# A gated recurrence and a mixture of experts on one core: products read in token order, row scatters freed of each other, and a new order table

## The chip, the cores and the metric

The kernel is one program on one core of a Trainium2 chip. The metric is the device time of one execution in microseconds; lower is better. The engines are named as the profile names them: PE (matmul; PEld is its weight load), DVE (vector), ACT (scalar), POOL (GpSimd) and SP (sync, which here issues most transfers).

## The reference

```python
# attention block: batch 4, 8 heads, 768 tokens, head size 48, float32
mag = sqrt(a_re*a_re + a_im*a_im); scale = minimum(mag, 0.999) / (mag + 1e-6)
a = (a_re + 1j*a_im) * scale                      # one complex gate per token, head and channel
for t in range(S):                                # state: 48 x 48 per batch and head
    St = a[t][:, None] * St + outer(k[t], v[t])
    y[t] = q[t] @ real(St)
x = y.transpose(0, 2, 1, 3).reshape(3072, 384)    # token rows
# experts: 8 experts, 384 -> 1024 -> 384, one expert per token, no token dropped
e = argmax(x @ w_gate, axis=1); g = softmax(x @ w_gate)[e]
out[n] = g[n] * (maximum(x[n] @ w1[e[n]], 0) @ w2[e[n]])
```

## The kernel before

**Attention.** The recurrence is computed in 24 blocks of 128 tokens: `u` counts the six chunks of the sequence, `b` the four batches, and a loop runs over `g = u*4 + b`. Once per `u`, logarithms, arctangents and two products with a triangular matrix (`csl`, `cst`) turn the gates into decays and rotations. Per block, `products` makes the rotated queries and keys `Q` and `K` on DVE; `scores` turns them on PE (`tp`), copies them out on ACT (`kt`, `qt`), multiplies them (`at`) and masks the result on DVE (`am`); `outer` and `state` keep the running state `G`; `results` adds two products for each head in the PSUM tile `yt`: `v` times `am`, and from the second chunk on `G` times `qt`. `evict` copies `yt` to `ys` on ACT, `finish` turns `ys` in 32 by 32 squares on DVE into `x`, and four transfers on SP's queue write `x` to the DRAM scratch `xd`, one row for each token. `logits` and `pick_logits` multiply `ys` with the gate weights.

**How `results` uses PE.** Two heads share a column of `yt`: head `i=0` writes partitions 0 to 47, head `i=1` partitions 64 to 111. The moving operand is a row of 128 tokens. It is read through

```python
def by_square(t):
    return t.rearrange("p (s j) -> p j s", j=CT)      # CT = 4
```

so that column `j*32+s` of `yt` is token `s*4+j` of the block, and the operand's consecutive reads lie four float32 apart. `at`, `tp` and all products of the experts read their moving operand without a gap. Since the columns stand in that order, so do the partitions of `lg`, `tid1` and `xid1`, and `finish` writes partition `s` to the rows `s*4 .. s*4+3`. A float32 matmul of the program shows as two MATMUL instructions in the trace: 192 calls with `am` are x384 in a row.

**Routing.** After chunk pairs, `route` ranks the tokens of each expert and sums their token numbers (`tid1`, `xid1`) into `slots`. `first_place` finds the expert with the most tokens (product `cnt`), after which SP loads that expert's `wa` and `wb`, and POOL gathers its first 256 rows `xg` from `xd`. Its first half (`hps`, `yps`) is computed while the last chunk is routed.

**Experts.** Each of eight experts takes its rows by indirect gathers on POOL, multiplies with `wa` (`hx`, `hy`, `hz`, `hv`, and `mx` to `mv` for the second product), scales by the gate into `y`, and `scatter` writes each `y` of up to 128 rows to `out` by one indirect transfer on POOL. There are 28 scatters and a last one. All write to the tensor `out`, so the framework puts them one after another: each waits for the landing of the one before. `drain` puts a POOL drain behind the scatters of experts 3 and 6, and later scatters behind it. The last `y` is held back: at the end every engine reads a flag and branches over a fallback path (the `If` at line 1282), then DVE scales the last 104 rows (`y<-mv,gate`) into a tile of the pool `lasty`, and the last scatter (`out_dram<-y,lasts`) ends the kernel.

**What sets the order.** All engine calls up to the end of the attention part are recorded (a helper at line 110 issues them, so all have that line). `ORDER` gives for each engine the sequence in which they run, as numbers of the recorded calls; the loop at line 1190 ties each to the next on its engine. The experts' part is ordered by the program and by chains of `behind`.

Of the kernel before, what the change touches and what calls it, by code (L numbers as in the profile page):

```python
# [48 lines left out]
    """,  # L49
    "scalar": """  # L50
# [9 lines left out]
    """,  # L60
    "vector": """
# [15 lines left out]
    """,  # L77
    "gpsimd": """
        3 21 17 7 0 18 16 6 11 25 23 13 1 19 10 20 9 2 26 5 4 28 22 27 29 12 30+1 14 32 34 8 33 35+1 38 24 40 15 37 39
        42 44 41 43 46 45 47+1  # L80
    """,
    "sync": """
# [48 lines left out]
def kernel(  # L131
# [42 lines left out]
    def behind(ins, others, reason="order"):  # L174
        for o in others:
            tc.add_manual_dep(ins.ins, o.ins.name, NOSYNC, reason=reason)
# [38 lines left out]
    tid1 = const([P, NU, B], "tid1")  # L215
    xid1 = const([P, NU, B], "xid1")
    for t, pattern in ((tid1, [[P, NU], [S, B]]), (xid1, [[B * P, NU], [P, B]])):
        for a in range(CT):
            nc.gpsimd.iota(
                t[a * Q4 : (a + 1) * Q4], pattern=pattern, base=1 + a, channel_multiplier=CT,  # L220
                allow_small_or_imprecise_dtypes=True,
            )
# [238 lines left out]
    def by_square(t):  # L461
        return t.rearrange("p (s j) -> p j s", j=CT)

    def results(u, b, hg):
        half, c = divmod(b, HB)
        V = T["v", u, half][:, c]
        for hp in range(2 * hg, 2 * hg + 2):
            o = [yt[i * 64 : i * 64 + D, hp].rearrange("p (j s) -> p j s", j=CT) for i in range(2)]
            for i in range(2):
                mm(o[i], V[:, 2 * hp + i], by_square(T["am", u, b, hg][:, 2 * (hp % 2) + i]), True, u == 0)  # L470
            for i in range(2):
                if u > 0:
                    mm(o[i], T["G", b][0:DD, 2 * hp + i], by_square(T["qt", u, b, hg][0:DD, 2 * (hp % 2) + i]), False, True)
# [20 lines left out]
    def finish(u, b):  # L494

        x = ch.tile([P, CT, Q4, HP], FP, tag="x", name="x")
        nc.vector.transpose(
            out=x.rearrange("p j s i -> p i j s"), in_=T["ys", u, b].rearrange("p i (j s) -> p i j s", j=CT)
        )
        rows = xd[(u * B + b) * P : (u * B + b + 1) * P, :].rearrange("(s j) c -> s j c", j=CT)  # L500
        for a in range(4):
            w = min(Q4, D - a % 2 * Q4)
            c0 = a // 2 * D + a % 2 * Q4
# [1065 lines left out]
```

## Time and profile before

| | |
|---|---|
| median of three runs | 567.14 us (561.68 to 567.54) |
| profiled execution | 566.88 us; span 565.1 us, that is 1.8 us around the span |
| PE | 537.3 us busy, 95% of the span |
| DVE | 384.0 us, 68% |
| ACT | 257.0 us, 45% |
| POOL | 173.4 us, 31% |
| mean granted TensorE clock | 0.991 |

Attention takes about the first 293 us: up to 40 us the first gates are loaded and turned, from 43.4 us on `yt` is written. The first half of the first expert follows to about 323 us, the rest of the experts to 553 us, and a tail without matmuls to 565 us. Matmuls are pipelined: the mean time of one contains its way through the array, and two neighbours overlap. What a matmul costs is read from starts, or from the busy time of a group divided by its count.

### The profile page before, as it was taken

The page shows a single profiled execution, that of the slowest core. Times are in us where ns is not written, and L with a number is a line of the kernel's source. Part 1 is how long each engine was busy: PE and PEld are TensorE (multiplying, and loading weights), DVE is VectorE, ACT ScalarE, POOL GpSimd, SP SyncE. Part 2 cuts the span into 40 slices and gives each one's busy share as a digit, 9 for nine tenths or more (in the row PEclk, how much of TensorE's full clock was granted, in tenths as well). Part 3 has the DMA queues.
Part 4 walks back from the last instruction along what each step waited for, and adds up shares of the span by engine and source line. Part 5 has one row for each costly group of instructions (what it writes and reads, how often), then busy time and mean ns, then how long its engine had stood idle before and what let it go on. Part 6 is the DMA issues. An engine that isn't in the chain of part 4 may idle for free. (4 is left out here: it accounts for less than half of the span.)

```text
span 565.1 us, 9630 instructions
## 1 busy us (share of the span) xinstructions
PE 537.3 (95%) x3626; PEld 427.2 (76%) x3626; DVE 384.0 (68%) x754; ACT 257.0 (45%) x424; POOL 173.4 (31%) x174
## 2 busy tenths in 40 slices
PE   4699999999999999999999999999999999999991
PEld 3487777777787867766758678888888989898990
DVE  4599776787898797777726527677576666665730
ACT  6797868574686875553321013232323313232320
POOL 1050120040031012000010566777538346146322
PEclk9999999999999999999999999999999999999997
DMA  9949667465753465331081197465453637371111
GB/s 166 172 67 135 133 116 142 76 108 103 143 93 71 75 131 78 69 73 29 16 267 29 41 369 273 158 223 185 134 213 111 245 134 265 128 252 42 42 56 40
DMA packets 173646, 73.51 MB, mean 130 GB/s; under 512 B 153677, under 2 KB 168039, under 8 KB 172696
## 3 DMA queue, kind: packets, MB, share of 16 engines
q1 hardware_dynamic: 168504, 63.05, 46.5%
q0 software_dynamic: 5088, 9.77, 5.7%
q8 instruction: 30, 0.49, 0.4%
q14 instruction: 24, 0.20, 0.1%
HBM read 63.30 MB, written 9.68 MB: 129 GB/s over the span
## 5 line engine op out<-in xcount | busy, mean ns | idle before, releaser
L110 POOL DMA_INDIRECT xg<-xd,tok x92 | 104.5, 1136 | 119.2 <-DVE am L110 64.7
L110 POOL TENSOR_SCALAR carry<-fg 32x768 f32<-32x768 f32 x10 | 23.9, 2392 | 176.2 <-DVE fg L110 176.0
L110 PE MATMUL yt<-am,v 128*48 128x128 f32 x384 | 67.9, 407 | 0.0
L110 PE MATMUL yt<-qt,G 96*48 96x128 f32 x320 | 62.5, 407 | 0.0
L110 POOL DMA_INDIRECT out_dram<-y,row x28 | 31.7, 1133 | 82.7 <-DMA out_dram<-y,row 25.3
L110 PEld LDWEIGHTS at<-qt,kt 96*128 96x128 f32 x384 | 47.4, 191 | 9.4 <-issue 6.0
L110 PE MATMUL at<-qt,kt 96*128 96x128 f32 x384 | 53.4, 281 | 0.2 <-ACT qt L110 0.2
L110 DVE TENSOR_TENSOR am<-at,tri 128x512 f32<-128x512 f32 x48 | 32.9, 685 | 22.3 <-PE at L110 19.5
L110 PE MATMUL mv<-wb,ht 128*128 128x384 f32 (+5 forms) x176 | 43.2, 488 | 0.0
L110 PEld LDWEIGHTS yt<-qt,G 96*48 96x48 f32 x320 | 28.8, 139 | 13.7 <-issue 1.7
L110 PEld LDWEIGHTS yt<-am,v 128*48 128x48 f32 x384 | 26.6, 132 | 15.2 <-issue 5.6
L110 ACT COPY kt<-tp 96x512 f32<-96x512 f32 x48 | 27.9, 582 | 18.9 <-PE tp L110 18.8
L110 ACT COPY qt<-tp 96x512 f32<-96x512 f32 x48 | 28.0, 583 | 16.4 <-PE tp L110 14.9
L110 PEld LDWEIGHTS mv<-wb,ht 128*128 128x128 f32 (+5 forms) x176 | 22.3, 156 | 15.8 <-issue 4.6
L110 PEld LDWEIGHTS dk<-v,K 128*96 128x96 f32 x320 | 30.1, 165 | 2.8 <-issue 1.9
L110 PE MATMUL dk<-v,K 128*96 128x48 f32 x320 | 30.8, 246 | 0.0
L110 PE MATMUL tp<-ident,Q 128*96 128x128 f32 x192 | 30.1, 276 | 0.5 <-ACT qt L110 0.2
L110 PE MATMUL tp<-ident,K 128*96 128x128 f32 x192 | 30.5, 276 | 0.0
L110 ACT ACTIVATE ht<-hv 128x192 f32<-128x192 f32 (+6 forms) x18 | 8.3, 461 | 46.1 <-PE hv L110 46.1
L110 DVE STREAM_TRANSPOSE x<-ys 128x512 f32<-128x512 f32 x24 | 26.7, 1114 | 3.2 <-ACT ys L110 3.1
L110 PE MATMUL hx<-xt,wa 128*128 128x192 f32 (+5 forms) x136 | 28.4, 334 | 0.2 <-DVE xt L110 0.2
L110 ACT COPY ys<-yt 128x512 f32<-128x512 f32 x24 | 14.1, 587 | 27.1 <-PE yt L110 27.1
(238 smaller groups left out, 1156.0 us busy)
## 6 DMA issues: line engine op xcount, KB each, us to landing
wb<-in_moe_w_dram SPq DMA_DIRECT2D x8, 1536.0 KB
wa<-in_moe_w_dram SPq DMA_DIRECT2D x7, 1536.0 KB
k<-in_k_dram SPq DMA_DIRECT2D x12, 384.0 KB
v<-in_v_dram SPq DMA_DIRECT2D x12, 384.0 KB
q<-in_q_dram SPq DMA_DIRECT2D x12, 384.0 KB
rc<-in_a_re_dram SPq DMA_DIRECT2D x6, 768.0 KB
rc<-in_a_im_dram SPq DMA_DIRECT2D x6, 768.0 KB
ar<-in_a_re_dram SPq DMA_DIRECT2D x9, 384.0 KB
```

Of the source, the lines that this page charges most:

```text
L110: ins = f(*a, **kw)
```

## The change

Five things change together.

1. `by_square` is gone: `results` reads `am` and `qt`, and writes `yt`, in the natural order of tokens. Column `j*32+s` is token `j*32+s`.
2. `finish` writes partition `s` of `x` to the rows `s`, `32+s`, `64+s`, `96+s` of the block. The pieces have the same sizes as before. `tid1` and `xid1` are made by one `iota` each instead of four.
3. All scatters are declared free of dependence on one another (a group "rows"). In the fallback path a drain waits for all of them.
4. The fallback path reads its rows in the same natural order.
5. `ORDER` is replaced for all five engines; its numbers name other calls where calls fell away.

```diff
-            o = [yt[i * 64 : i * 64 + D, hp].rearrange("p (j s) -> p j s", j=CT) for i in range(2)]
+            o = [yt[i * 64 : i * 64 + D, hp] for i in range(2)]
             for i in range(2):
-                mm(o[i], V[:, 2 * hp + i], by_square(T["am", u, b, hg][:, 2 * (hp % 2) + i]), True, u == 0)
+                mm(o[i], V[:, 2 * hp + i], T["am", u, b, hg][:, 2 * (hp % 2) + i], True, u == 0)
             for i in range(2):
                 if u > 0:
-                    mm(o[i], T["G", b][0:DD, 2 * hp + i], by_square(T["qt", u, b, hg][0:DD, 2 * (hp % 2) + i]), False, True)
+                    mm(o[i], T["G", b][0:DD, 2 * hp + i], T["qt", u, b, hg][0:DD, 2 * (hp % 2) + i], False, True)
...
-        rows = xd[(u * B + b) * P : (u * B + b + 1) * P, :].rearrange("(s j) c -> s j c", j=CT)
+        rows = xd[(u * B + b) * P : (u * B + b + 1) * P, :].rearrange("(j s) c -> s j c", j=CT)
...
+    tid1 = iota([[P, NU], [S, B]], "tid1", base=1, cm=1)
+    xid1 = iota([[B * P, NU], [P, B]], "xid1", base=1, cm=1)
...
         if "drained" in T:
             behind(ins, [T["drained"]])
+        tc.declare_no_dep(ins.ins, group="rows", reason="rows of different tokens")
+        tc.add_to_no_dep_group("rows", ins.ins)
+        T["rows"] = T.get("rows", []) + [ins]
         T["scattered"] = ins
...
     with tc.If(nc.values_load(flag[0:1, 1:2], min_val=0, max_val=P * (NC + 1)) > 0):
         gp = ExitStack()
+        behind(nc.gpsimd.drain(), T["rows"], "rows written", SYNC)
...
-        3 21 17 7 0 18 16 6 11 25 23 13 1 19 10 20 9 2 26 5 4 28 22 27 29 12 30+1 14 32 34 8 33 35+1 38 24 40 15 37 39
-        42 44 41 43 46 45 47+1
+        8 5 7 10 3 17 19 11 4 20 22 21 24 12 23 25 2 9 26 28 27 29 15+1 1 6 0 30 18 32 13 34 31 33 36 35 37+1 40 39 14
+        41+1
```

Two places show what the order becomes. The first is PE late in the attention part, in the last chunk but one block from its end: `cnt` is the product after which the first expert is known, so its weights can be loaded, and `at`, `tp`, `yt`, `lt` belong to the last blocks. Before:

```order
L110 MATMUL sp<-ohi,olo 128x3x32 x4
L110 MATMUL tp<-ident,K 96x128 x3
L110 MATMUL at<-qt,kt 128x128
L110 MATMUL cnt<-acc,ones 128x8
L110 MATMUL at<-qt,kt 128x128 x3
L110 MATMUL tp<-ident,K 96x128
L110 MATMUL lt<-pick,ls 128x8
L110 MATMUL tp<-ident,Q 96x128 x2
L110 MATMUL yt<-am,v 48x128 x2
```

And of the change:

```order
L109 MATMUL sp<-ohi,olo 128x3x32 x4
L109 MATMUL at<-qt,kt 128x128 x4
L109 MATMUL cnt<-acc,ones 128x8
L109 MATMUL tp<-ident,K 96x128 x3
L109 MATMUL lt<-ys,wg 32x128 x4
L109 MATMUL yt<-am,v 48x128
L109 MATMUL tp<-ident,K 96x128
L109 MATMUL yt<-am,v 48x128
```

`cnt` stands at nearly the same place: in both programs 32 products into `yt` follow it before the first `hps`. What moved is that products into `yt` now begin sooner after `cnt`, with score products spread between them.

The second place is POOL's end: the last five scatters ahead of the `If` (three of expert 6, two of expert 7), with the semaphores that each waits for. `DMASW` are the eight semaphores that POOL's own transfers raise in turn, so that the one a transfer raises was last raised eight transfers earlier. Before:

```order
L110 DMA out_dram<-y,row 3072x384 [waits DMASW5_49,DMASW4_49,Activation_49]
L110 DMA out_dram<-y,row 3072x384 [waits DMASW5_49,DMASW6_49,DVE_49,Activation_49]
L110 DMA out_dram<-y,row 3072x384 [waits DMASW6_49,Activation_49]
L110 DMA out_dram<-y,row 3072x384 [waits DMASW7_49,DVE_49,Activation_49]
L110 DMA out_dram<-y,row 3072x384 [waits DMASW0_49,Activation_49]
```

And of the change:

```order
L109 DMA out_dram<-y,row 3072x384 [waits DMASW5_49,Activation_49]
L109 DMA out_dram<-y,row 3072x384 [waits DMASW6_49,DVE_49,Activation_49]
L109 DMA out_dram<-y,row 3072x384 [waits DMASW7_49,Activation_49]
L109 DMA out_dram<-y,row 3072x384 [waits DMASW0_49,DVE_49,Activation_49]
L109 DMA out_dram<-y,row 3072x384 [waits DMASW1_49,Activation_49]
```

The first of these five raises `DMASW5`, the last `DMASW1`. Before, each waits for the semaphore of the scatter just ahead of it (`DMASW4`, `5`, `6`, `7`, `0`), that is for its landing. In the change each waits only for the last use of its own, eight transfers back, and for its data.

More of the change, by code (lines that the diff above doesn't have):

```diff
@@ L172, in mm, with behind @@
         return T["mm"]
-    def behind(ins, others, reason="order"):
+    def behind(ins, others, reason="order", how=NOSYNC):
         for o in others:
-            tc.add_manual_dep(ins.ins, o.ins.name, NOSYNC, reason=reason)
+            tc.add_manual_dep(ins.ins, o.ins.name, how, reason=reason)
     cp = ctx.enter_context(tc.tile_pool(name="cp", bufs=1))
@@ L214 @@
     ifl = iota([[P, CT - 1]], "ifl", base=P)
[L215 to L222, printed above, removed]
+    tid1 = iota([[P, NU], [S, B]], "tid1", base=1, cm=1)
+    xid1 = iota([[B * P, NU], [P, B]], "xid1", base=1, cm=1)
     wg = const([P, HP, Q4], "wg")
@@ L459, in outer @@
             T["dk", b] = dk
-    def by_square(t):
-        return t.rearrange("p (s j) -> p j s", j=CT)
     def results(u, b, hg):
@@ L1365 @@
                     x = xl.tile([P, DM], FP, tag="x", name="x")
-                    rows = xf[b * S + u * P : b * S + (u + 1) * P, :].rearrange("(s j) d -> j s d", j=CT)
-                    for a in range(CT):
-                        nc.sync.dma_start(out=x[a * Q4 : (a + 1) * Q4], in_=rows[a])
+                    nc.sync.dma_start(out=x, in_=xf[b * S + u * P : b * S + (u + 1) * P, :])
                     tp = psZ.tile([P, KD, P], FP, tag="mm", padded_shape=[P, 4, P], name="tpx")
```

95 rows, old and new, of the table ORDER are left out of this document.

## The prediction

> **What bounds the kernel now.** I read the page first, then busy time by stretch, then the same for the tile `yt` alone, then the groups of PE, then its timeline.
>
> ```profile
> span 565.1 us, 9630 instructions
> PE 537.3 (95%) x3626; PEld 427.2 (76%) x3626; DVE 384.0 (68%) x754; ACT 257.0 (45%) x424; POOL 173.4 (31%) x174
> ```
>
> PE is busy nearly all the time, but a busy PE need not be a PE at its best rate. By stretch (columns: PE, PEld, DVE, ACT, POOL busy, granted clock, DMA share, GB/s):
>
> ```profile
> 40.00:285.00 245.00, 244.77 (x2034) 180.77 (x2034) 193.03 (x336) 157.76 (x226) 26.66 (x22) 1.00 0.52 93
> 285.00:323.00 38.00, 36.90 (x198) 25.73 (x192) 18.91 (x96) 3.72 (x10) 8.65 (x9) 0.96 0.41 121
> 323.00:553.00 230.00, 229.02 (x1269) 200.52 (x1268) 146.03 (x271) 64.32 (x143) 125.18 (x109) 1.00 0.50 174
> 553.00:565.10 12.10, 0.28 (x1) 0.00 (x0) 0.62 (x1) 0.00 (x0) 2.99 (x3) 0.73 0.13 44
> ```
>
> From 40 to 285 us, the body of the attention part, PE is busy 244.8 of 245 us, DVE 193.0, ACT 157.8. So PE sets this stretch, and who waits confirms it (DVE and ACT in the same stretch: engine and tile waiting, releaser, us, times, longest):
>
> ```profile
> DVE am L110 <- PE at L110: 19.5, 13, 2.5
> DVE x L110 <- ACT ys L110: 3.1, 2, 2.4
> DVE fg L110 <- ACT fg L110: 2.8, 2, 1.5
> DVE K L110 <- ACT CS L110: 1.0, 2, 0.7
> ACT ys L110 <- PE yt L110: 23.3, 16, 3.1
> ACT kt L110 <- PE tp L110: 18.8, 16, 2.9
> ```
>
> The long waits are for PE; those of DVE for ACT sum to 3.1 + 2.8 + 1.0 = 6.9 us. The experts (323 to 553 us) are PE's as well, with 229.0 of 230 us, and the change does not touch their products. The last 12 us have no matmuls.
>
> **The products into `yt`.** The same stretches with `yt` alone, then groups of PE (line, tile, stationary shape, moving shape, count, busy us, mean ns of one):
>
> ```profile
> 40.00:285.00 245.00, 90.01 (x656) 45.57 (x658) 0.00 (x0) 12.91 (x22) 1.00 0.52 93
> 285.00:323.00 38.00, 6.12 (x52) 3.20 (x46) 0.00 (x0) 1.17 (x2) 0.96 0.41 121
> ```
>
> ```profile
> L110 PE MATMUL yt<-am,v 128*48 128x128 f32 x384 | 67.9, 407 | 0.0
> L110 PE MATMUL yt<-qt,G 96*48 96x128 f32 x320 | 62.5, 407 | 0.0
> L110 PE MATMUL tp<-ident,Q 128*96 128x128 f32 x192 | 30.1, 276 | 0.5 <-ACT qt L110 0.2 <-DVE Q L110 0.2
> L110 PE MATMUL mv<-wb,ht 128*128 128x384 f32 x80 | 26.6, 486 | 0.0
> L110 PE MATMUL lt<-ys,wg 128*32 128x128 f32 x192 | 9.7, 280 | 0.4 <-ACT ys L110 0.4
> L110 PE MATMUL my<-wb,ht 128*64 128x384 f32 x16 | 2.8, 492 | 0.0
> ```
>
> Each of the 704 instructions into `yt` takes 407 ns; `tp` and `lt`, which also stream 128 columns, take 276 and 280. The timeline says how they follow one another (start us, length, engine, tile, count):
>
> ```profile
> 199.80 1.16 PE L110 MATMUL at<-qt,kt 96*128 96x128 f32 x8
> 200.89 0.64 PE L110 MATMUL yt<-am,v 128*48 128x128 f32 x4
> 201.35 0.64 PE L110 MATMUL yt<-qt,G 96*48 96x128 f32 x4
> 201.81 0.64 PE L110 MATMUL yt<-am,v 128*48 128x128 f32 x4
> ```
>
> From 200.89 to 201.81 stand eight instructions, that is four pairs (heads `i=0` and `i=1`): 0.92 / 4 = 0.23 us for a pair. Two halves of the array do run side by side: `my`, with 64 of the columns, needs 2.8 / 16 = 0.175 us each, half of the 26.6 / 80 = 0.333 us that `mv` needs for as many tokens with the full width. A pair without gaps thus costs what one full instruction costs: 0.333 / 384 x 128 = 0.111 us by columns. `at` needs (200.89 - 199.80) / 8 = 0.136 us with its turn to the next tile, `tp` 30.1 / 192 = 0.157 us busy, and `lt` sets four side by side in 9.7 / 48 = 0.20 us. What sets `yt` apart from these is the moving operand read four floats apart.
>
> **The change part by part.** 704 / 2 = 352 pairs. From 0.23 us to x each: x = 0.111 saves 41.9 us, x = 0.157 saves 25.7 us. I take 0.115, since `yt` comes in long rows like `mv`: **40 us less PE work**, 37 of it from 40 to 285 us (656 instructions) and 3 after.
>
> [...]
>
> How much of the 37 us reaches the clock on the wall? PE alone would bring the stretch from 245 to 208 us. DVE's 193.0 us in it do not shrink, so DVE goes from 79% to 93%, ACT from 64% to 76%, the transfers from 0.52 to 0.61 of the DMA engines. Of DVE's 15 us that are left, 6.9 are the waits for ACT. Two engines that hand results to and fro in fixed order will not both be full; I give back 5 us, so the stretch becomes 213 us: **-32 us**. Bounds: 0 given back, or DVE at 85% busy, which is 227 us and only -18.
>
> After 285 us the early expert takes over:
>
> ```profile
> 280.33 0.35 PE L110 MATMUL cnt<-acc,ones 128*128 128x8 f32 x2
> 283.48 0.65 SPq L110 DMA_DIRECT2D wa<-in_moe_w_dram  x1
> 284.98 1.37 SPq L110 DMA_DIRECT2D wa<-in_moe_w_dram  x2
> 295.55 8.33 PE L110 MATMUL hps<-xt,wa 128*128 128x256 f32 x30
> ...
> GB/s 166 172 67 135 133 116 142 76 108 103 143 93 71 75 131 78 69 73 29 16 267 29 41 369 273 158 223 185 134 213 111 245 134 265 128 252 42 42 56 40
> ```
>
> From `cnt` to `hps` are 15.2 us, with 32 products into `yt` in both orders, 64 instructions or 32 pairs, so 32 x 0.115 = 3.7 us less: 11.5 us. The weights `wa` are issued up to 6 us after `cnt`; the 21st of the page's 40 slices, which holds them, moved 267 GB/s, at which 1.5 MB take 5.9 us. That is just in time, so of the 3 us I count **-2**.
>
> **The scatters.** The end, with the time between two scatters on POOL:
>
> ```profile
> 518.49 1.03 POOL L110 DMA_INDIRECT out_dram<-y,row  x1 [0.30 <-ACT p5g L110]
> ...
> 544.56 1.01 POOL L110 DMA_INDIRECT out_dram<-y,row  x1 [2.65 <-DMA out_dram<-y,row]
> 547.95 0.98 POOL L110 DMA_INDIRECT out_dram<-y,row  x1 [2.37 <-DMA out_dram<-y,row]
> 553.65 0.99 POOL L110 DMA_INDIRECT out_dram<-y,row  x1 [4.72 <-issue]
> 557.02 0.98 POOL L110 DMA_INDIRECT out_dram<-y,row  x1 [2.38 <-DMA out_dram<-y,row]
> 560.75 1.02 POOL L110 DMA_INDIRECT out_dram<-y,lasts  x1 [2.75 <-DMA out_dram<-y,row]
> ...
> 524.95 0.42 ACT L110 ACTIVATE y<-mz,gate 128x192 f32<-128x192 f32 x1 [4.30 <-PE mz L110]
> 548.16 0.42 ACT L110 ACTIVATE y<-mz,gate 128x192 f32<-128x192 f32 x1 [3.48 <-PE mz L110]
> 547.96 5.33 PE L110 MATMUL mv<-wb,ht 128*104 128x384 f32 x16
> 558.69 0.62 DVE L110 TENSOR_SCALAR y<-mv,gate 104x384 f32<-104x384 f32 x1 [11.41 <-DMA out_dram<-y,row]
> ```
>
> Each scatter costs 3.4 us, of which POOL works 1.0. Expert 6's last `y` is ready at 525.37 us, but its scatters leave up to 547.95, and the 4.7 us before 553.65 hold the drain. PE is done at 553.29 and DVE's last `y` starts at 558.69: it stands behind POOL's passage through the `If`. Without the waits a scatter costs about 1.3 us (1.0 and a gap of 0.3, as ahead of the one at 518.49, which follows a gather). The backlog at 518.5 us, nine scatters up to the drain, is then gone by about 530, the drain by 540 even at twice its 4.7 us, and expert 7's second scatter leaves at 548.9, right behind its data. From the last scatter ahead of the `If` to DVE's last `y` are 558.69 - 557.02 = 1.7 us now, so POOL is through by about 550.6, before PE ends. So the last `y` starts at 553.3 instead of 558.7, and the last scatter needs no wait for a landing: **-6 us**. Bounds: -4, if the drain grows to 15 us; -6.5.
>
> **At nothing.** The rows of `x` go out in pieces of the same size, from the same partitions, at a DMA share of 0.52; the six `iota` less lie on POOL, for which nobody waits early. The new order: PE has 0.2 us idle from 40 to 285, so there is nothing to win there, and what it may lose I bound at 6 us, the same as it might win in the start up to 40 us.
>
> **The sum** goes against the profiled execution, 566.9 us (the median of 567.1 is 0.2 above it, well inside the 1% that a measurement of this kernel can tell from no change): 566.9 - 32 - 2 - 6 = **527 us**.
>
> **Rivals.**
> - *DVE becomes the bound* (0.13). PE's rows above speak for it, with 93% asked of DVE; against it, that most of DVE's waits were for PE. At 85% the stretch is 227 us: 566.9 - 18 - 2 - 6 = 541 us.
> - *The stride is free* (0.06), and a pair of 48 columns takes 0.23 us for another reason, such as its weight loads. Only the scatters pay: 566.9 - 6 = 561 us. Against it: `my` and `lt` load as often, and run at full rate.
> - *The scatters still wait* (0.06), on the semaphore's last use or the drain: 527 + 6 = 533 us.
> - *Slower: PE cools* (0.03). Where PE idled, its granted clock fell:
>
> ```profile
> 280.00:300.00 20.00, 18.90 (x141) 12.82 (x140) 7.50 (x34) 3.40 (x8) 2.19 (x2) 0.91 0.57 190
> ```
>
> 1.1 us of idle time, spread over a few waits, cost 0.09 of the clock of that stretch. If PE waits for DVE in every block, each pause slows the products behind it. The place is 40 to 285 us; the price is 208 us divided by the clock. It turns the sign where that exceeds 245 + 8, at a mean clock under 0.82; at 0.80 the stretch is 260 us and the kernel 574.
>
> **The numbers.** The forecast has 0.72, and its own range, 515 to 538 us, comes from the bounds (0 to 11 us given back, or x = 0.157 us in their place; 6 us of order; 2 us of tail). With the rival of the scatters and half of DVE's, 514 to 543 holds 0.72 + 0.06 + 0.06 = 0.84. Faster by over 1% (under 561.4): forecast, DVE, scatters and a third of the free stride, 0.93. Same: the rest of the free stride, 0.04. Slower: 0.03.
>
> **What would show it.** In the changed profile: `yt` at about 275 ns each and its busy time near 50 us instead of 90.0 + 6.1 = 96; PE still busy from 40 us on, with DVE above 88% of the stretch; `yt` last written near 258 us; scatters 1.3 us apart where they queue, and the last `y` within 0.3 us of PE's end. Wrong would be: `yt` still at 407 ns (the stride was not it); `yt` short, but DVE without idle time and PE waiting for `am` or `Q` (I gave back too little); a granted clock under 0.95 in the attention part.

## The result, and the profile after

The changed kernel takes 527.88 us in the median of four runs (527.14 to 530.2), the kernel before beside it 566.42 us: a ratio of 0.934, 95% interval 0.928 to 0.940. The forecast was 527.0 us in a range of 514 to 543. The profiled execution took 527.66 us, its span 525.7 us.

The page of the changed kernel, then its busy time by stretch (PE, PEld, DVE, ACT, POOL busy, granted clock, DMA share, GB/s):

```profile
span 525.7 us, 9611 instructions
PE 500.6 (95%) x3626; PEld 419.8 (80%) x3626; DVE 383.6 (73%) x754; ACT 255.3 (49%) x424; POOL 170.3 (32%) x168
```

```profile
40.00:248.00 208.00, 207.19 (x2032) 171.78 (x2026) 190.62 (x338) 155.05 (x223) 26.04 (x26) 1.00 0.62 109
248.00:287.00 39.00, 34.15 (x191) 25.03 (x191) 19.48 (x94) 4.31 (x11) 6.27 (x7) 0.93 0.38 116
287.00:514.00 227.00, 226.09 (x1254) 199.57 (x1253) 146.38 (x271) 63.92 (x142) 126.32 (x113) 0.99 0.51 177
514.00:526.00 12.00, 5.87 (x21) 3.10 (x19) 0.62 (x1) 0.42 (x1) 3.00 (x3) 0.92 0.15 50
```

PE still sets the body of the attention part, with 207.2 of 208 us, and DVE is now at 191 us, 92%. The transition, 248 to 287 us, is new: PE idles 5 us there, where it idled 1.1 us in as long a stretch before. The products into `yt`, by group and on the timeline:

```profile
L109 PE MATMUL yt<-am,v 128*48 128x128 f32 x384 | 42.8, 280 | 0.3 <-ACT ys L109 0.3
L109 PE MATMUL yt<-qt,G 96*48 96x128 f32 x320 | 37.1, 274 | 0.0
...
226.32 0.39 PE L109 MATMUL yt<-qt,G 96*48 96x128 f32 x4
226.54 0.39 PE L109 MATMUL yt<-am,v 128*48 128x128 f32 x4
226.76 0.39 PE L109 MATMUL yt<-qt,G 96*48 96x128 f32 x4
```

Rows of two pairs start 0.22 us apart: a pair takes 0.11 us, where it took 0.23. That is 352 x 0.12 = 42 us less. The end of PE, of POOL's scatters and of DVE:

```profile
514.54 5.32 PE L109 MATMUL mv<-wb,ht 128*104 128x384 f32 x16
514.64 0.99 POOL L109 DMA_INDIRECT out_dram<-y,row  x1 [19.38 <-DVE y L109]
515.94 0.98 POOL L109 DMA_INDIRECT out_dram<-y,row  x1 [0.30 <-issue]
520.06 0.62 DVE L109 TENSOR_SCALAR y<-mv,gate 104x384 f32<-104x384 f32 x1 [6.19 <-PEq L1275]
```

POOL waits for data now, its two queued scatters are 1.3 us apart, and DVE's last `y` follows PE's end (519.9 us) by 0.2 us. In the transition PE waits for other engines and for a gather (engine and tile waiting, releaser, us, times, longest):

```profile
PE tp L109 <- DMA xg<-xd,tok: 2.0, 1, 2.0
PE hy L109 <- DVE bad L109: 1.8, 1, 1.8
```

The stages of four kernels, from the starts of PE's instructions in their traces (us). The last two columns are experiments told below, the second run of the old order and the version with `tok` first:

| stage | before | changed | old order | old order, `tok` first |
|---|---|---|---|---|
| span's start to first `yt` | 43.4 | 39.6 | 42.9 | 43.5 |
| first to last `yt` | 248.8 | 212.8 | 207.9 | 209.0 |
| last `yt` to first `hy` | 28.3 | 32.1 | 31.2 | 26.5 |
| first `hy` to last `mv` | 232.3 | 234.9 | 231.0 | 230.9 |
| last `mv` to span's end | 12.3 | 6.3 | 6.3 | 6.3 |
| span | 565.1 | 525.7 | 519.2 | 516.2 |

From before to changed that is 3.8 us less in the start, 36.0 less between the `yt`, 3.8 more in the transition, 2.6 more in the experts and 6.0 less in the tail: 39.4 us less in all.

One thing has to be known for the first four experiments: on the chip that they ran on, the stage from `hy` to the last `mv` took 267 to 276 us instead of 231 to 237, and the kernel of before, which ran beside them, 604.14 us; so they are read by ratio, and by the other stages.

### The profile page after: what moved, and what is told of

Same layout as the page of the kernel before. It is cut to its first block, busy times and chain, and to the rows that moved or that the text cites. A ratio compares the mean times of both kernels' runs of the same rounds, so it can differ in the third digit from the quotient of the medians.

```text
span 525.7 us, 9611 instructions
## 1 busy us (share of the span) xinstructions
PE 500.6 (95%) x3626; PEld 419.8 (80%) x3626; DVE 383.6 (73%) x754; ACT 255.3 (49%) x424; POOL 170.3 (32%) x168
## 5 line engine op out<-in xcount | busy, mean ns | idle before, releaser
L109 POOL DMA_INDIRECT xg<-xd,tok x92 | 103.0, 1119 | 112.3 <-DVE am L109 54.6
L109 PE MATMUL yt<-am,v 128*48 128x128 f32 x384 | 42.8, 280 | 0.3 <-ACT ys L109 0.3
L109 PE MATMUL yt<-qt,G 96*48 96x128 f32 x320 | 37.1, 274 | 0.0
L109 ACT COPY kt<-tp 96x512 f32<-96x512 f32 x48 | 27.9, 581 | 12.3 <-PE tp L109 12.2
L109 PE MATMUL dk<-v,K 128*96 128x48 f32 x320 | 31.2, 247 | 0.0
L109 PEld LDWEIGHTS yt<-am,v 128*48 128x48 f32 x384 | 24.6, 122 | 7.6 <-issue 3.5
L109 PE MATMUL hx<-xt,wa 128*128 128x192 f32 (+5 forms) x136 | 29.5, 343 | 0.4 <-DVE xt L109 0.4
L109 PEld LDWEIGHTS hx<-xt,wa 128*128 128x128 f32 x136 | 23.8, 196 | 3.7 <-issue 2.5
L109 PEld LDWEIGHTS tp<-ident,K 128*96 128x96 f32 x192 | 20.7, 128 | 6.0 <-issue 4.0
```

Of the source, the lines that this page charges most:

```text
L109: ins = f(*a, **kw)
```

## The experiments

**1. The old order, with the other parts of the change.**

```diff
 ORDER = {
-    "tensor", "scalar", "vector", "sync": the new rows
+    "tensor", "scalar", "vector", "sync": the rows of before
     "gpsimd": the new row
```

> The change with the order of before for the PE, ACT, DVE and SP (the POOL keeps the changed order, since calls of its own fell away): contiguous reads and free scatters, without the new order. Theory A (the shorter pair of yt and the six freed scatters carry the gain, the order only trims): the yt pair costs 0.11 us and the scatters stand 1.3 us apart as in the changed kernel, only the start (3.8 us earlier in the changed kernel) and some waits for the DVE are lost, so 530 to 538 us. Theory B (the old order was made for long pairs, and with short ones the PE waits for the DVE at every turn; the new order makes the gain): the yt pair is 0.11 us all the same, but the stretch from 40 to 285 us stays near its old length, 550 us or more.

Measured: 562.68 us, ratio to before 0.934 (0.927 to 0.941), the same as the changed kernel elsewhere; in us it is 41.5 below the kernel of before there, where the changed kernel was 38.5 below. The pair took 0.11 us. The absolute number lies in theory B's range and outside theory A's, for the reason just given; the other stages say more. First to last `yt` took 207.9 us, against 248.8 before and 212.8 in the new order, so theory B is out: the new order did not make the gain, and it may even cost. I ran this kernel again (experiment 10).

**2. The new order and the free scatters, with the stride.**

```diff
...  # o: the same columns, seen in groups of 32
-    mm(o[i], V[:, 2 * hp + i], T["am", u, b, hg][:, 2 * (hp % 2) + i], True, u == 0)
+    mm(o[i], V[:, 2 * hp + i], T["am", u, b, hg][:, 2 * (hp % 2) + i].rearrange("p (s j) -> p j s", j=4), True, u == 0)
...  # qt likewise
```

> The changed kernel, except that the products of results read am and qt at every fourth float again (the rows of a block of 128 tokens then come out in another order, so the output is permuted inside each block; the amount of work is the same). Theory A (the stride is the cost): the yt pair goes back from 0.11 to 0.23 us, 352 pairs x 0.12 = 42 us of PE work come back, of which what the DVE had cost falls away: 559 to 568 us. Theory B (the order is what made the gain): under 540 us, with the pair at 0.23 us hidden in waits.

Measured: 599.71 us, ratio 0.993 (0.990 to 0.997). The groups of `yt` are back where they were:

```profile
L109 PE MATMUL yt<-am,v 128*48 128x128 f32 x384 | 71.2, 407 | 0.3 <-ACT ys L109 0.3
L109 PE MATMUL yt<-qt,G 96*48 96x128 f32 x320 | 63.7, 407 | 0.0
```

First to last `yt` took 255.2 us, 42.4 more than in the changed kernel. With only the stride put back, 0.7% against before is left of the 6.6%. The absolute numbers missed on this chip; by ratio and by stages theory A holds.

**3 and 4. The scatters: freed ones made to wait again, and freed ones alone.**

```diff
 # 3, from the changed kernel
-        tc.declare_no_dep(ins.ins, group="rows", reason="rows of different tokens")
-        tc.add_to_no_dep_group("rows", ins.ins)
 # 4, from the kernel of before
+        tc.declare_no_dep(ins.ins, group="rows", reason="rows of different tokens")
+        tc.add_to_no_dep_group("rows", ins.ins)
+        behind(nc.gpsimd.drain(), T["rows"], "rows written", SYNC)   # ahead of the rest
```

> The changed kernel without the declaration that the scatters of rows do not depend on one another (the drain behind them stays). Theory A (the last scatters stand on the path, six waits of 2.4 to 2.9 us in the tail of before): the last scatters are 3.5 to 4.1 us apart again instead of 1.3, the last multiplication of y ends 6 us after the PE's end instead of 0.3 us, 533 to 535 us. Theory B (the tail got short for another reason, the new order, and the scatters are hidden): within 1 us of 528 us.

> The kernel of before with one part of the change alone: the scatters of rows are declared free of one another, and a drain on the POOL stands ahead of the rest that reads them. Theory A (the freed scatters are worth their place in the tail whatever goes ahead of them): 560 to 562 us, 6 us less than before, all of it behind the start of the last mv. Theory B (the freed scatters are worth something only with the new order, or the drain takes the gain back): 565 to 567 us.

Measured: the third 562.86 us, ratio 0.930 (0.925 to 0.936); the fourth 602.53 us, ratio 0.998 (0.994 to 1.002). In times, neither part shows: the changed kernel itself was not run on this chip, but the third's ratio agrees with that of experiment 1, which has the free scatters; and theory A's 6 us would make the fourth's ratio 0.990, outside its interval. The last scatters of the third, then of the fourth (start, length, engine, what, idle time ahead and its releaser):

```profile
551.28 0.99 POOL L109 DMA_INDIRECT out_dram<-y,row  x1 [17.29 <-DVE y L109]
556.07 0.98 POOL L109 DMA_INDIRECT out_dram<-y,row  x1 [3.80 <-DMA out_dram<-y,row]
560.32 1.02 POOL L109 DMA_INDIRECT out_dram<-y,lasts  x1 [3.27 <-DMA out_dram<-y,row]
...
591.43 0.98 POOL L110 DMA_INDIRECT out_dram<-y,row  x1 [19.38 <-DVE y L110]
592.73 0.99 POOL L110 DMA_INDIRECT out_dram<-y,row  x1 [0.30 <-issue]
597.76 1.02 POOL L110 DMA_INDIRECT out_dram<-y,lasts  x1 [4.05 <-DVE y L110]
```

With waits they are 4.8 and 4.2 us apart, and from the last `mv` to the end are 9.0 us; freed, they are 1.3 us apart (the last one waits for its data), and the tail is 5.9 us in the fourth, with every order of before, and 6.3 us in the changed kernel. So freeing them is worth 2.7 us in this tail, with 17.3 us of idle time ahead of the last three. In the profile of before, which ran undisturbed, seven scatters stood in a row from 537 us on, and the tail was 12.3 us. The slow expert of this chip shifts PE against POOL and may have let the backlog drain early; the kernel of before was not profiled there. POOL's new row is no rival: `ORDER` ends with the attention part, and behind it the traces of before and changed have POOL's instructions in the same sequence, but for one scatter that stands two places earlier; in the fourth, where only the scatters were freed, it does too. That the tail fell by 6.0 us is measured; whether the waits account for all of it was not tried in an undisturbed run.

**5. The changed kernel once more.** No edit.

> The changed kernel itself once more, beside the others. In the four runs before this one, the stretch from hy to the last mv took 267 to 276 us instead of 232 to 235, and the kernel of before 604 us instead of 566, while every other stage had its length. Theory A (the chip of those runs slowed the PE at the first expert, whatever the kernel): the changed kernel has its stages as recorded first outside that stretch (first yt to last yt 212.8 us, last yt to hy 32 us, tail 6 us), and on that chip 562 to 568 us, on one like the first 526 to 530 us. Theory B (the four edits brought the slow stretch in): 526 to 530 us on the same chip, with 604 us for before.

Measured: 527.22 us, ratio 0.933 (0.930 to 0.936), on a chip where the kernel of before took 566.12 us. Stages outside the expert as first recorded (first to last `yt` 212.8 us, transition 31.9, tail 6.3). This run was not on the chip of the first four, so it doesn't decide between the two theories; for A speaks that the unedited kernel of before took 604.14 us there, and that experiment 4, whose stages up to `hy` are those of before to 0.1 us, met the same slow expert.

**6 and 12. Other strides.** Same edit as in 2, with `j=2` and `j=8`.

> The changed kernel with the products of results reading am and qt at every second float (rows of output permuted inside each block of 128 tokens, the same amount of work). [...] Theory B (any gap between floats halves the rate): the pair is 0.23 us as it was at every fourth float, first to last yt about 249 to 255 us. [...]

> The changed kernel with the products of results reading am and qt at every eighth float (rows of output permuted inside each block of 128 tokens, the same amount of work). At every second float the pair of yt took 0.11 us (276 ns each, 273 when contiguous), at every fourth 0.23 us. [...] Theory B (the cost grows with the gap): 0.35 us or more a pair, first to last yt 285 us or more.

Measured: every second float 528.47 us, every eighth 571.48 us (one time each; before beside them 566.12 and 565.32). The tile's instructions (min/median/max ns, first and last start), at two, then at eight, and the timeline at eight:

```profile
L109 PE MATMUL yt<-am,v x384: 273/276/317, 38.0 to 252.0; 128*48 128x128 f32 x192
...
L109 PE MATMUL yt<-am,v x384: 408/412/417, 39.8 to 296.2; 128*48 128x128 f32 x192
...
226.60 0.41 PE L109 MATMUL yt<-am,v 128*48 128x128 f32 x1
226.61 0.64 PE L109 MATMUL yt<-qt,G 96*48 96x128 f32 x2
226.84 0.41 PE L109 MATMUL yt<-am,v 128*48 128x128 f32 x1
227.07 0.41 PE L109 MATMUL yt<-qt,G 96*48 96x128 f32 x1
```

At two floats apart the pair costs 0.115 us, little above the 0.11 of contiguous reads (first to last `yt` took 214.3 us, 1.5 more); at four and at eight it costs 0.23 and 0.235 us (two pairs from 226.60 to 227.07). It is a step between two and four, nearly flat behind it, so theory B is out in both: at two the pair did not go to 0.23 us, and at eight not to 0.35. At eight, first to last `yt` took 256.9 us, 7 us more than the 250 that I had estimated for a pair of 0.23 us and 1.7 more than in experiment 2, and the kernel 42.5 us more than the changed one beside it, where I had estimated 33 to 37. What makes the step was not shown: no stride of three and no other type was run.

**7. Some calls of the transition moved, in the new order.**

```diff
-        for x in range(3):
+        for x in (2, 1, 0):          # tokens of the first expert
...
+        by_place(gate, 1)            # ahead of fj instead of behind it
# ORDER: DVE's chain from key to own0 ahead of a transpose and a mask product,
# the held y ahead of the rows' bookkeeping, PE's sq inside the second yps
```

> The changed kernel with a few calls of the transition moved: the first tokens of experts are looked for with expert 0 last in the loop but its chain on the DVE ahead of a transpose and a mask multiplication; the gate is placed ahead of fj, and the held y is scaled ahead of the rows' bookkeeping; the product sq stands in the middle of the second yps. Theory A (the PE's two waits in the transition, 2.0 us for expert 0's gather and 1.75 us for the DVE's chain ahead of hy, are order alone): both go or halve, last yt to hy 32.1 us becomes 28 to 30 us, the kernel 2 to 4 us less than the changed kernel run beside it. Theory B (the DVE is full there, what is moved ahead only makes another wait late): within 1 us of the changed kernel, with new waits of 2 us or more for kt, qt or am.

Measured: 526.66 us, ratio 0.926 (0.922 to 0.930), the changed kernel beside it 0.933 (0.930 to 0.936): 0.6 us in medians, but two of six runs took 521 us, and the ratios differ by 0.7%, with intervals that just overlap. The two waits fell as theory A said (the gather's is gone, `hy`'s is 0.7 us) and last `yt` to `hy` fell to 27.4 us; but first to last `yt` rose from 212.8 to 219.3 us. PE's new wait, and the 10.5 us behind it:

```profile
PE at L110 <- DVE pr L110: 1.6, 1, 1.6
PE hy L110 <- DVE y L110: 0.7, 1, 0.7
...
248.00:258.50 10.50, 10.50 (x78) 8.76 (x78) 1.83 (x6) 1.43 (x3) 0.86 (x2) 0.51 0.97 300
```

A wait of 1.6 us was traded in, and PE, fully busy behind it, ran 10.5 us at a granted clock of 0.51: 5.1 us lost. By the medians that is theory B's time, by the ratios theory A's, so the time decides nothing; the new wait, 1.6 us and not the 2 us or more of theory B, is of the kind that B had said, and the clock behind it is a term that neither had.

**8. More work for DVE.**

```diff
+        more = tc.nc.vector.reduce_max(spare, bc(tri, 1, 4), axis=AX_X)   # behind each block's transpose
...  # tied into DVE's order there
```

> The changed kernel with 24 more instructions on the DVE in the stretch of the blocks, one behind each block's transpose, each a maximum over 128x512 of tri of about 0.69 us: 16.5 us of DVE work that nobody needs. In the changed kernel the DVE is busy 191 of the 208 us there (92%), the PE 207. Theory A (the PE bounds the stretch, the DVE has room left): first to last yt grows by 2 to 6 us. Theory B (the DVE became the bound): it grows by 12 to 17 us, and the PE's idle time in front of at, tp or yt names the DVE.

Measured: 531.71 us, ratio 0.939 (0.936 to 0.941), 4.5 us above the changed kernel beside it; first to last `yt` 215.6 us, 2.8 more. The 24 instructions took 626 ns each, 15.0 us together:

```profile
L493 DVE TENSOR_REDUCE spare<-tri x24: 615/626/645, 49.2 to 269.7; 128x4 f32<-128x512 f32 x24
...
40.00:248.00 208.00, 205.50 (x2001) 169.67 (x2003) 199.43 (x346) 155.47 (x223) 26.04 (x26) 1.00 0.59 109
```

DVE took the work at 96% busy, and PE lost 1.7 us of its busy time in the stretch. DVE at 92% was not the bound: theory A.

**9. The changed kernel a third time**, for the three beside it. No edit.

> The changed kernel a second time, to stand beside the three others on one chip. Its time hangs on how many stretches of 3.4 us at half clock follow the PE's two waits in the transition: 524 to 530 us where the first expert's stretch isn't slowed, with first yt to last yt 212.8 us and last yt to hy 32 us; if this chip slows the first expert as the first four runs showed it, 560 to 568 us.

Measured: 529.0 us, ratio 0.934 (0.932 to 0.937), before beside it 565.32.

**10. The old order again.** The edit of experiment 1.

> The changed kernel with the order of before for the PE, ACT, DVE and SP, a second time, since in its first run the first expert was slowed on every kernel. Theory A (the new order gives nothing, the stretch of the blocks with contiguous reads is shorter in the old order: 207.9 us from first to last yt against 212.8, and hy starts 1 to 3 us earlier): 520 to 525 us, 2 to 6 us less than the changed kernel beside it. Theory B (the first run's stages were an accident of that chip; the new order is worth its start of 2.5 to 4 us): 529 to 534 us, more than the changed kernel.

Measured: 520.8 us (519.95 to 521.21), ratio 0.920 (0.918 to 0.923). The intervals are apart: the new order costs 8.2 us against the old one beside it, and theory A holds, with more than the 2 to 6 us that it said.

**11. The old order, with DVE's `tok` ahead.**

```diff
 -        for x in range(3):
+        for x in (2, 1, 0):          # calls 363 and 364 are now those that tok needs
...
# DVE's row of the old order (call numbers)
-        356 385 357 358 359 360 361 362 363 378 364 365 366 367 368 370 401
+        356 357 358 359 363 364 370 385 360 361 362 378 365 366 367 368 401
```

356 adds to `slots`, 357 is `key`, 363 and 364 look up the token numbers (in the old loop they were 367 and 368), 370 writes `tok`, 385 is the transpose of `x`, 360 to 362 make `own0`.

> The old order as in the run before this one, and in it on the DVE the chain from cnt to tok ahead of a transpose of x and of own0's three instructions: the gather of expert 0's rows is issued some 1.6 us earlier. Theory A (the PE's one wait left in the transition, 2.4 us for that gather, is the place of tok in the DVE's row): the wait falls to 1 us or less, fewer half-clock stretches follow it, and the kernel is 1.5 to 4 us below the old order beside it: 517 to 522 us. Theory B (the gather lands when the loads of wa and wb let it, at 340 to 380 GB/s): the landing stays where it was, within 1 us of the old order.

Measured: 517.89 us (517.46 to 518.03), ratio 0.915 (0.913 to 0.918): the fastest of all, 2.9 us below the old order and 11.1 us below the changed kernel. The longest wait of PE from 240 us to `hy`, and the stretch from 252 to 262 us, first in the old order, then here:

```profile
PE tp L112 <- DMA xg<-xd,tok: 2.4, 1, 2.4
252.00:262.00 10.00, 7.11 (x32) 5.53 (x25) 3.04 (x13) 1.02 (x3) 0.00 (x0) 0.66 0.67 241
...
PE lt L112 <- DVE lg L112: 1.1, 1, 1.1
252.00:262.00 10.00, 8.90 (x61) 7.38 (x58) 5.22 (x20) 2.31 (x7) 0.00 (x0) 1.00 0.82 281
```

`tok` was written at 244.7 instead of 245.8 us, the gather issued at 245.80 instead of 246.85. PE, held up 1.1 us by `lg`, came to the rows 1.6 us later and found them there. The transposes `tp` began 0.8 us earlier; from there to `hy` PE needed 24.4 instead of 26.6 us, with the clock at 1.00 instead of 0.66. By these figures the clock's part of the 3 us is larger than the wait's.

## Why the prediction was right, and where it was right by accident

- **The pair.** Right: 0.23 to 0.11 us against the 0.115 that I had estimated from the 0.111 of `mv`, 42 us less PE work against 40. In the trace, the time from each `yt` to the next start, summed between first and last `yt`, went from 91.8 to 49.7 us. Shown by experiments 2, 6 and 12: 0.23 us at every fourth float, 0.115 at every second, 0.235 at every eighth. Why it steps there is not shown.
- **"I give back 5 us" because DVE gets full.** The size came out (first to last `yt` fell by 36.0 us, of 42 us that PE was spared, so 6 were given back), the reason did not. With 15 us more on DVE the stretch grew by 2.8 us, and with the old order it fell by 40.9 us at the same DVE load (191.2 of 208 us from 40 to 248): 42.4 us of `yt` with only 1.5 us given back. In the new order, 8 instructions of `at`, 16 of `dk` and 8 of `tp` stand behind the first `yt` that stood ahead of it; by their start-to-start times 3.6 us more than in the old order. Most of the give-back is that work, which the earlier start pushed behind it, and not a full DVE. That start, 3.8 us earlier and counted at nothing, is also why `yt` was last written at 252.6 us and not near 258.
- **"-2" in the transition.** Wrong: from `cnt` to `hps`, the stretch that I counted, 1.1 us were won (15.2 to 14.1), and from `hps` to `hy` 1.7 lost; last `yt` to `hy` grew by 3.8 us. I took the weights `wa` for what `hps` waits for, and did not look at the gather of the rows, nor at when PE comes to `hy`. With `yt` short PE is there before the gather lands (2.0 us) and, at `hy`, before DVE's chain of placing (1.8 us). The old order met only the first (2.4 us), and last `yt` to `hy` grew by 2.9 us; with `tok` ahead, `cnt` to `hps` took 12.4 us. Behind the changed kernel's two waits the granted clock was 0.50 for 3.4 and for 6.8 us, that is 1.7 and 3.4 us of full clock besides the 2.0 and 1.8 us of the waits themselves.
- **"-6" in the tail.** Right: last `mv` to end fell by 6.0 us, the last `y` stands 0.2 us behind PE, and the scatters stand 1.3 us apart. What the waits alone cost undisturbed was not tried (experiments 3 and 4).
- **The order "at nothing", bounded at 6 us.** The step that failed: it costs 8.2 us (experiments 9 and 10). In the two profiled executions, 8.7 us apart, it wins 3.1 us up to the first `yt`, gives these and 1.8 us more back by the last `yt`, and loses 0.9 us in the transition and 5.9 us in the experts (2.9 and 4.0 us against the other two profiles of the changed kernel), where PE waits 2.2 us for DVE's `xt` and the clock falls twice (the wait, then two windows of experiment 9):

```profile
PE hx L109 <- DVE xt L109: 2.2, 1, 2.2
284.00:292.00 8.00, 7.30 (x28) 4.79 (x29) 1.90 (x7) 0.65 (x2) 5.51 (x6) 0.79 0.28 67
306.00:314.00 8.00, 6.42 (x25) 6.02 (x26) 4.46 (x10) 2.00 (x4) 6.17 (x7) 0.79 0.97 329
```

- **The sum.** 527 came out because errors cancelled. With the old order's stages for the terms, first `yt` to `hy` gains 38 us where I said 32 + 2, that is 4 us more; start and experts gain 2 us that I had at nothing; the order, counted at nothing, takes 8 us: 527 - 4 - 2 + 8 = 529 us, what experiment 9 measured. The rival of DVE as the bound is refuted (2.8 us more between the `yt` for 15 us more on DVE), as is the free stride (0.11 us a pair without it, 0.23 with it put back). That PE cools was a rival priced for the attention part, where the clock was 1.00; here its place is the transition (0.93 from 248 to 287 us) and the first expert (0.58 from 284 to 292 us).

## What to carry to other kernels

Look at the stride of a product's moving operand before anything else when its instructions take half again as long as others of the same shape (407 ns against 276): here floats four apart cost twice (0.23 against 0.11 us a pair), two apart next to nothing (0.115). When one engine's work in a stage shrinks by a sixth, look at each place where it hands over to a chain on another engine; here it then arrived early, and behind a wait of 2.0 us stood 3.4 us at half clock, 1.7 us more. And measure each part of a change alone, the order table too: here the part that looked like fitting the rest cost 8 us.

## What the runs showed of the hardware that I had not expected

**Half clock in steps.** In the traces of before and changed PE's granted clock is 1.00 or 0.50, and between the blocks and the last `mv` the halves last 3.4 us (before, from 295.6 us; changed, from 257.9 us) and 6.8 us (changed, from 285.2 us). Experiment 7 had a mean of 0.51 over 10.5 us, experiment 10 one of 0.66 over 10 us, as much as 10.3 and 6.8 us at half. They stand behind single waits of 1.6 to 2.4 us (2.0 and 1.8 us in the changed kernel, 1.6 in experiment 7, 2.4 in experiment 10), and in the kernel of before behind three short ones of 1.1 us in all. It is not certain that one follows: experiment 11, with the same three and 1.1 us more, had none (1.00 from 248 to 282 us), and the changed kernel, profiled three times with the same wait of 1.7 to 1.8 us ahead of `hy`, had 6.8, 0 and 3.4 us of half clock behind it (0.58, 1.00 and 0.79 over 8 us); in the second, a wait of 2.3 us for `xt` was not followed by one either (1.00 from 287 to 514 us). The first and the second of these, around `hy`:

```profile
284.00:292.00 8.00, 7.54 (x20) 5.03 (x21) 1.65 (x6) 0.32 (x1) 5.75 (x6) 0.58 0.30 76
282.00:290.00 8.00, 7.40 (x37) 5.90 (x38) 2.16 (x8) 0.84 (x3) 5.61 (x6) 1.00 0.41 130
```

PE began 20 matmul instructions in the one and 37 in the other. Runs of the changed kernel spread over 524.8 to 530.5 us and those of experiment 11, with no wait over 1.1 us there, over 0.6 us. That the clock makes this spread is not shown: of the 5.1 us between the shortest and the longest of the three profiles 1.9 lie ahead of the first `yt`, and of the five runs of experiment 10 the two with the lowest mean clock (0.983 and 0.984) were the fastest. What brings a stretch of half clock about is not shown.

**A slow expert on one chip.** In experiments 1 to 4 first `hy` to last `mv` took 267 to 276 us instead of 231 to 237. In experiment 3 PE, ACT and DVE did little for about 30 us of it, at the first expert, while POOL's gathers went on:

```profile
292.00:326.00 34.00, 15.34 (x50) 10.55 (x49) 6.46 (x14) 1.14 (x4) 26.38 (x26) 0.71 0.41 133
```

PE signalled the ends of its rows of six matmul instructions at 293.9, 295.4, 298.3, 303.2 and 311.0 us, where the changed kernel has them 1.0 us apart: the steps between them grow from 1.5 to 7.8 us, nearly eight times. The granted clock of 0.71 does not account for that. What causes it was not tried; it met all four kernels profiled on that chip and none of those profiled elsewhere.
